# Block attention and two expert layers: four widths for an expert's first products, PSUM tiles cleared in a row and kept for two groups, and twelve transposes at one place

## Chip, cores and metric

The kernel runs on one core of a Trainium2 chip. The metric is the time of one execution on the device, in microseconds (us); the time of a kernel is the median of several executions.

## What is computed

An attention over 4 batches, 8 heads, 576 positions and 64 dimensions (masked, half of the heads local, half strided) gives x with 2304 tokens of 512 dimensions. A first expert layer sends every token to one of 8 experts, which has two matrices, 512 x 1024 and 1024 x 512. A second layer does causal attention once per expert, for 4 experts, and adds up each token's two chosen ones. The change lies in the first expert layer:

```
for s in range(S):
    fresh_e = int(np.argmax(logits[b, s]))
    if s == 0 or local_gate[b, s] < 0.5:
        e = fresh_e
    else:
        e = prev_e if prev_e >= 0 else fresh_e
    prev_e = e
    ...
    h = np.maximum(x[b, s] @ w1[e], 0.0)
    out[b, s] = p[e] * (h @ w2[e])
```

How many tokens an expert gets is known only at run time. On the reference's inputs it is 294, 311, 363, 357, 267, 269, 209 and 234 for experts 0 to 7.

## The kernel before

Every fp32 product is made of three matmuls: both operands are split into a high and a low part (`split`, L118 on ScalarE and L119 on VectorE), and `mm3` (L122 to L124) adds high x high, high x low and low x high in PSUM. The program has three stretches: attention, routing and expert 0 up to about 160 us, the loop over experts 1 to 7 up to about 390 us, and the second layer.

In the loop, one expert `e` (1 to 6) goes through these steps:

- `h_step(e, f)` for f = 0 to 7, one *group* each: 128 of the 1024 inner columns, as the product of `W1` (four tiles of 128 input dimensions) and the expert's transposed tokens `XH[e]`; 4 x 3 = 12 matmuls into a PSUM tile `hp` of 384 columns, one column a token. How many columns are computed is decided on TensorE by a count `CN[e]` that `load_cn` reads: 384, 320 or 256 (`EARLY`). The columns beyond are cleared by `zero` (L849), one bf16 matmul. Then `relu2` (L704 on ScalarE, L705 on VectorE) makes the high and low part of the result from all 384 columns. The tiles `hp` use the PSUM tags s (two buffers), s, xt and lg in turn, so that group f + 4 uses the buffer of group f.
- `split_w2(e, f)` beside it: the high and low part of a 128 x 512 piece of the second matrix.
- `y_step(e, r)` for r = 0, 1, 2, 128 tokens each: 8 x 3 matmuls of 512 columns into `yp`, scaled by ScalarE and scattered to memory by GpSimd. For r = 2 an expert with fewer tokens does a shorter form or clears the tile only.
- Beside `y_step(e, 1)`, `xt_expert(e + 1, [c])` transposes the next expert's gathered tokens, 128 dimensions (c) at a time: three transposes on TensorE into a tile `xp` (L841), and its split into `XH[e + 1]`. `next_w` splits pieces of the next expert's first matrix (`w1h`, `w1l`).

Expert 7 takes another path (`h_late`, `hpl`). TensorE and GpSimd follow the order in which the program is written; ScalarE, VectorE and the DMA queue of SyncE follow an order that a scheduler made from it.

Of the kernel before, what the change touches and what calls it, by code (L numbers as in the profile page):

```python
# [9 lines left out]
FT = mybir.dt.float32  # L10
# [46 lines left out]
def kernel(  # L57
# [19 lines left out]
    DM = H * D  # L77
    NE, _, F = moe_w1.shape
# [3 lines left out]
    CAP = 384  # L82
    RC = CAP // 128
    EARLY = 256
# [8 lines left out]
    def pool(c, name, bufs=1, **kw):  # L93
        return c.enter_context(tc.tile_pool(name=name, bufs=bufs, **kw))
# [56 lines left out]
    def shared(n, shape, dt, name):  # L151
        return sh.tile(shape, dt, name=name, tag=f"sh{n}", bufs=1)
# [568 lines left out]
    for n in range(NU * B):  # L721
# [10 lines left out]
        m = n + 2  # L732
# [13 lines left out]
    for b in range(B):  # L746
        o = 4 * b + 5
        t = (.1, .57, .58, .85, .88, 1.25, 1.58, 1.9, 2.15, 2.5, 2.58) if b < B - 1 else RL
        r = [(logits, (b, (0, 1))), (logits, (b, (2, 3)))]
# [19 lines left out]
    psum = pool(ctx, "psum", space=PSUM)  # L769
# [60 lines left out]
    def xt_expert(e, cs=range(4)):  # L830
        if 0 not in cs:
            pass
        elif e % 2:
            XH[e] = [bp.tile([128, 4, CAP], FR, name=f"xo{n}", tag=f"xo{n}", bufs=1) for n in range(2)]
        else:
            XH[e] = [shared(n, [128, 4, CAP], FR, f"xh{n}") for n in range(2)]
        h, l = XH[e]
        for c in cs:
            p = psum.tile([128, CAP], FT, name="xp", tag="prep", bufs=2)
            for r in range(RC):  # L840
                nc.tensor.transpose(p[:, r * 128:(r + 1) * 128], XG[e, r][:, c * 128:(c + 1) * 128], idf)  # L841
            split(h[:, c], l[:, c], p)

    CN = {}
# [4 lines left out]
    def zero(o):  # L849
        nc.tensor.matmul(o, zb, zb[:, :1].to_broadcast([128, o.shape[1]]), start=True, stop=True)  # L850

    def h_step(e, f):
        nt = EARLY if e == NE - 1 else CAP
        tag = ("s", "s", "xt", "lg")[f % 4]
        p = psum.tile([128, CAP], FT, name="hp", tag=tag, bufs=2 if tag == "s" else 1)[:, :nt]
        xh, xl = XH[e]
        def body(n):
            for c in range(4):
                wh, wl = W1[e, c]
                fs = slice(f * 128, (f + 1) * 128)  # L860
                mm3(p[:, :n], wh[:, fs], wl[:, fs], xh[:, c, :n], xl[:, c, :n], c == 0, c == 3)
            if n < nt:
                zero(p[:, n:])

        if nt > EARLY:
            with tc.If(CN[e] > 320) as q1:
                body(CAP)
            with q1.Else():
                with tc.If(CN[e] > EARLY) as q2:
                    body(320)  # L870
                with q2.Else():
                    body(EARLY)
        else:
            body(nt)
        if f == 0:
            HT[e] = [bp.tile([128, 8, CAP], FR, name=f"h{n}", tag=f"ht{n}", bufs=1) for n in range(2)]
        relu2(HT[e][0][:, f, :nt], HT[e][1][:, f, :nt], p)
# [46 lines left out]
        split(ht[0][:, n * 4:n * 4 + 4], ht[1][:, n * 4:n * 4 + 4], p)  # L924

    def y_step(e, r, beside={}, to=(0, 1)):
        p = psum.tile([128, DM], FT, name="yp", tag=("et", "pv", "lg")[r], bufs=1)
        late = e == 0 and r == 2
        hh, hl = HT["late" if late else e]
        rs = slice(0, 128) if late else slice(r * 128, (r + 1) * 128)  # L930
        def body():
            for f in range(8):
                wh, wl = W2[e, f]
                mm3(p, hh[:, f, rs], hl[:, f, rs], wh, wl, f == 0, f == 7)
                if f in beside:
                    beside[f]()

        def halves():
            for f in range(8):
                for w in range(2):  # L940
                    nc.tensor.matmul(p, HT["hl"][:, f], W2[e, f][w], start=f == w == 0, stop=f == 7 and w == 1)

        half = r == 2 and 0 < e < NE - 1
        if half:
            with tc.If(CN[e] > EARLY + 64) as c:
                body()
            with c.Else():
                with tc.If(CN[e] > EARLY) as c2:
                    halves()
                with c2.Else():  # L950
                    zero(p)
        elif r == 2 and e:
            with tc.If(CN[e] > EARLY) as c:
                body()
            with c.Else():
                zero(p)
        else:
            body()
        if e not in YS:
            YS[e] = shared(4, [128, RC, DM], FT, "y")  # L960
        y = YS[e][:, r]
        nc.scalar.activation(y, p, AF.Copy, scale=pslot[:, r, e:e + 1])  # L962
        if half:
            yb = bp.tile([64, DM], FT, name="yb", tag="hs", bufs=1)
            nc.scalar.activation(yb, p[64:], AF.Copy, scale=both[64:, e:e + 1])
            nc.vector.scalar_tensor_tensor(y[:64], yb, pslot[:64, r, e:e + 1], y[:64], op0=OP.mult, op1=OP.add)
        scatter(y, lambda n: sidx[:, n, r, e:e + 1], to)
# [135 lines left out]
    for e in range(1, NE):  # L1103
        if e + 1 < NE:
            gather(e + 1)
        if e == NE - 1:
            NOV.append(nc.values_load(nov, min_val=0, max_val=(NT - CAP) // 128))
            for f, a, ws in ((h_late, (0, 0), (0, 1, 2)), (h_late, (0,), (3,)), (h_late, (1,), ()),
                             (h_late, (1, 0), (4, 5)), (h_late_t, (0,), ()), (h_late_t, (1,), ()),
                             (h_late_t, (0, 0), ()), (h_late, (0, 1), (6, 7)), (h_late_t, (1, 0), ())):  # L1110
                for w in ws:
                    split_w2(e, w)
                f(e, *a)
            overflow()
            y_step(e, 2)
            y_step(e, 0, to=(0,))
            c_load(0)
            h_late(e, 1, 1)
            scatter(YS[e][:, 0], lambda n: sidx[:, n, 0, e:e + 1], (1,))
            h_late_t(e, 0, 1)  # L1120
            h_late_t(e, 1, 1)
            y_step(e, 1, to=(1,))
            for t in range(5):
                c_t(0, t)
            break
        for f in range(8):
            h_step(e, f)
            split_w2(e, f)
        if e in (1, 3):
            load_cw(e - 1)  # L1130
            load_cw(e)
        HT["hl"] = bp.tile([128, 8, 128], FR, name="h2", tag="hs", bufs=1)
        for x in range(2):
            nc.gpsimd.tensor_copy(HT["hl"][:, :, 64 * x:64 * x + 64], HT[e][x][:, :, EARLY:EARLY + 64])
        load_w2(e + 1)
        for r in range(RC):
            if r == 1:
                load_cn(e + 1)
            y_step(e, r, {2 * c: lambda c=c: xt_expert(e + 1, [c]) for c in range(4)} if r == 1 else {})
            next_w(e + 1, r)  # L1140
        if e + 2 < NE:
            load_w1(e + 2)
# [224 lines left out]
    for b in range(B):  # L1367
        P = TAB[b == B - 1]
        o = 20 * b
        for u in range(10):  # L1370
            pr, i = cunits[10 * b + u][1:]
# [15 lines left out]
    for i in ORD2 or range(len(ev)):  # L1387
        _, f, a = ev[i]
# [31 lines left out]
```

## Time and profile before

| | before |
|---|---|
| median of 3 executions | 600.62 us (600.55 to 603.41) |
| profiled execution | 601.53 us, span of its instructions 599.7 us |
| mean granted TensorE clock | 0.983 |
| TensorE (PE) busy | 566.1 us, 94% |
| VectorE (DVE) busy | 384.8 us, 64% |
| ScalarE (ACT) busy | 349.3 us, 58% |
| GpSimd (POOL) busy | 147.8 us, 25% |

PE stands for TensorE's matmuls, PEld for its weight loads, which lie beside them. Matmuls overlap: a row's second number is the length of an instruction, and what the engine takes per matmul is the distance from one start to the next. In rows of a timeline the columns are start, length, engine, line, operation, the tiles written and read, shapes, and how many instructions are merged in the row.

### The profile page before, as it was taken

The numbers are of one execution on the slowest core, as the hardware profiler recorded it, in microseconds if no ns is written. First come the engines' busy times: TensorE is split into PE (matmuls) and PEld (weight loads), VectorE is DVE, ScalarE is ACT, GpSimd is POOL, SyncE is SP. The second block draws the span as 40 slices with busy tenths as digits, with TensorE's granted clock in tenths as the row PEclk, the third lists the DMA queues.
The fourth block names the chain that finished last, engine by engine and source line by source line (L and its number), as shares of the span: only waits on it lengthen the run. The fifth ranks groups of instructions, "written<-read, shape, count | busy, mean of one in ns | idle before, by whom it ended". The sixth has DMA issues, their size and how long they took to land. (4 is left out here: it accounts for less than half of the span.)

```text
span 599.7 us, 14224 instructions
## 1 busy us (share of the span) xinstructions
PE 566.1 (94%) x5265; PEld 488.3 (81%) x5265; DVE 384.8 (64%) x1135; ACT 349.3 (58%) x868; POOL 147.8 (25%) x229
## 2 busy tenths in 40 slices
PE   7898899879899999999999999998999999999996
PEld 4787787668788898989898987798997997989764
DVE  3456788846474643475555555148897897887891
ACT  2575766641464653455555557335776767767883
POOL 8242223241341423335252534200000000000000
PEclk9699799999999999999999999998999999999999
DMA  9999979440685474584737330331302402302302
GB/s 182 171 242 255 228 184 244 156 147 4 221 283 156 177 236 126 185 263 155 228 131 219 117 144 15 105 108 31 98 18 67 137 19 58 94 37 58 93 18 89
DMA packets 81219, 82.47 MB, mean 138 GB/s; under 512 B 56808, under 2 KB 56808, under 8 KB 80624
## 3 DMA queue, kind: packets, MB, share of 16 engines
q1 hardware_dynamic: 73024, 65.58, 39.8%
q0 software_dynamic: 8112, 15.76, 7.7%
q8 instruction: 55, 0.90, 0.6%
q14 instruction: 28, 0.23, 0.1%
HBM read 62.42 MB, written 21.76 MB: 140 GB/s over the span
## 5 line engine op out<-in xcount | busy, mean ns | idle before, releaser
L196 POOL DMA_INDIRECT yd<-y,sidx x47 | 53.8, 1144 | 82.6 <-ACT y L962 52.3
L119 DVE TENSOR_TENSOR w1l<-w1raw,w1h 128x1024 fp32r<-128x1024 f32 (+1 forms) x44 | 42.3, 986 | 30.5 <-ACT w1h L118 30.5
L1248 ACT ACTIVATE E<-cs,c_mx 128x288 f32<-128x288 f32 (+4 forms) x96 | 45.7, 481 | 17.1 <-DVE c_mx L1246 14.6
L122 PE MATMUL yp<-w2h,h 128*128 128x512 f32 x128 | 52.8, 412 | 0.4 <-ACTq L972 0.4
L1278 POOL MEMSET E<- 128x128 f32 x40 | 8.3, 209 | 180.0 <-PE cet L1297 84.9
L118 ACT ACTIVATE w1h<-w1raw 128x1024 fp32r<-128x1024 f32 (+1 forms) x44 | 34.3, 828 | 28.6 <-PE hp L124 18.5
L124 PE MATMUL yp<-w2h,h 128*128 128x512 f32 x128 | 50.3, 393 | 0.0
L123 PE MATMUL yp<-w2l,h 128*128 128x512 f32 x128 | 50.0, 390 | 0.0
L119 DVE TENSOR_TENSOR w2l<-w2raw,w2h 128x512 fp32r<-128x512 f32 x56 | 35.7, 685 | 12.0 <-ACT w2h L118 5.8
L122 PE MATMUL qkp<-y,cw 128*128 128x288 f32 x128 | 39.1, 306 | 0.5 <-DVE y L119 0.5
L1241 PE MATMUL cs<-qkt 128*128 128x288 f32 (+4 forms) x192 | 38.5, 319 | 1.1 <-ACT E L1248 0.9
L1246 DVE TENSOR_REDUCE c_mx<-cs 128x1 f32<-128x288 f32 (+4 forms) x80 | 37.7, 484 | 1.2 <-PE cs L1241 0.7
L118 ACT ACTIVATE w2h<-w2raw 128x512 fp32r<-128x512 f32 x56 | 32.4, 631 | 9.4 <-PE yp L124 4.5
L124 PE MATMUL qkp<-y,cw 128*128 128x288 f32 x128 | 37.8, 295 | 0.0
L123 PE MATMUL qkp<-y,cw 128*128 128x288 f32 x128 | 37.7, 294 | 0.0
L705 DVE SCALAR_TENSOR_TENSOR h<-hp,h 128x384 fp32r<-128x384 f32 x48 | 25.0, 552 | 14.5 <-ACT h L704 14.5
L962 ACT ACTIVATE y<-yp,pslot 128x512 f32<-128x512 f32 x22 | 14.9, 682 | 31.5 <-PE yp L124 22.9
L1292 PE MATMUL cet<-idf,E 128*128 128x128 f32 x160 | 28.3, 279 | 5.0 <-ACT et L115 2.1
L122 PE MATMUL hp<-xo,w1h 128*128 128x320 f32 (+1 forms) x96 | 31.7, 331 | 0.0
L1241 PEld LDWEIGHTS cs<-qkt 128*128 128x128 f32 x192 | 28.7, 193 | 3.2 <-ACT E L1248 2.5
L190 POOL DMA_INDIRECT xg<-xd,gidx x24 | 24.4, 1017 | 26.1 <-DVE gidx L648 19.1
L122 PE MATMUL hp<-xh,w1h 128*128 128x384 f32 (+2 forms) x96 | 30.8, 321 | 0.0
(364 smaller groups left out, 1722.7 us busy)
## 6 DMA issues: line engine op xcount, KB each, us to landing
w1raw<-in_moe_w_dram SPq DMA_DIRECT2D x32, 512.0 KB
w2raw<-in_moe_w_dram SPq DMA_DIRECT2D x56, 256.0 KB
yr<-yd SPq DMA_DIRECT2D x20, 256.0 KB
qkt<-qkt SPq DMA_DIRECT2D x8, 576.0 KB
out_dram<-co SPq DMA_DIRECT2D x16, 256.0 KB
raw<-in_q_dram SPq DMA_DIRECT2D x16, 144.0 KB
raw<-in_k_dram SPq DMA_DIRECT2D x16, 144.0 KB
raw<-in_q_dram SPq DMA_DIRECT2D x8, 288.0 KB
```

The costliest lines, as they stand in the source:

```text
L118: nc.scalar.activation(hi, src, AF.Copy)
L119: (eng or nc.vector).tensor_tensor(lo, src, hi.bitcast(FT), op=OP.subtract)
L122: nc.tensor.matmul(o, ah, bh, start=start, stop=False, **kw)
L123: nc.tensor.matmul(o, ah, bl, start=False, stop=False, **kw)
L124: nc.tensor.matmul(o, al, bh, start=False, stop=stop, **kw)
L190: nc.gpsimd.indirect_dma_start(out=t, out_offset=None, in_=xd[:rows], in_offset=bass.IndirectOffsetOnAxis(ap=gidx[:, r, e:e + 1], axis=0))
L196: nc.gpsimd.indirect_dma_start(out=yds[n], out_offset=bass.IndirectOffsetOnAxis(ap=ix(n), axis=0), in_=y, in_offset=None, bounds_check=yds ...
L705: nc.vector.scalar_tensor_tensor(lo, p, 0.0, hi.bitcast(FT), op0=OP.max, op1=OP.subtract)
L1241: nc.tensor.matmul(o[:, h - h0], T[:, h, q0:q0 + 128], T[:, 2 + 2 * x + h, k0:k1], start=x == 0, stop=x == 1, skip_group_check=True)
L1246: nc.vector.tensor_reduce(mx[:, n, h0:h0 + G], o, axis=AX.X, op=OP.max, negate=True)
L1248: nc.scalar.activation(E[:, h, k0:k1], o[:, h - h0], AF.Exp, bias=mx[:, n, h:h + 1], accum_out=sm[:, n, h:h + 1])
L1292: nc.tensor.transpose(p[:, kt * 128:kt * 128 + 128], E[:, kt * 128:kt * 128 + 128], idf)
```

## The change

- The widths are 256, 288, 320 and 384, chosen by two comparisons in every case (before, the 384-wide arm was chosen after one).
- An expert's four tiles `hp` are allocated once, at f = 0. If the width is below 384, four zeros in a row clear the columns beyond it in all four tiles, ahead of the first group's products; group f + 4 writes to the same tile again, and its cleared columns stay as they are.
- All twelve transposes of the next expert stand after f = 3 of `y_step(e, 1)`, instead of three each after f = 0, 2, 4 and 6; from expert 2 on their tiles use the tags prep and s in turn (two buffers each) instead of prep alone.
- `y_step(e, 2)` uses the PSUM tag et (pv for expert 7) instead of lg.

```
-            p = psum.tile([128, CAP], FT, name="xp", tag="prep", bufs=2)
+            p = psum.tile([128, CAP], FT, name="xp", tag=("prep", "s")[c % 2 if e > 1 else 0], bufs=2)
...
+    HP = {}
+
     def h_step(e, f):
         nt = EARLY if e == NE - 1 else CAP
-        tag = ("s", "s", "xt", "lg")[f % 4]
-        p = psum.tile([128, CAP], FT, name="hp", tag=tag, bufs=2 if tag == "s" else 1)[:, :nt]
+        if f == 0:
+            for i, tag in enumerate(("s", "s", "xt", "lg")):
+                HP[i] = psum.tile([128, CAP], FT, name="hp", tag=tag, bufs=2 if tag == "s" else 1)
+        p = HP[f % 4][:, :nt]
         xh, xl = XH[e]
         def body(n):
+            if n < nt and f == 0:
+                for i in range(4):
+                    zero(HP[i][:, n:])
             for c in range(4):
                 wh, wl = W1[e, c]
                 fs = slice(f * 128, (f + 1) * 128)
                 mm3(p[:, :n], wh[:, fs], wl[:, fs], xh[:, c, :n], xl[:, c, :n], c == 0, c == 3)
-            if n < nt:
-                zero(p[:, n:])
+
+        def pick(ws):
+            if len(ws) == 1:
+                body(ws[0])
+                return
+            m = len(ws) // 2
+            with tc.If(CN[e] > ws[m - 1]) as q:
+                pick(ws[m:])
+            with q.Else():
+                pick(ws[:m])
 
         if nt > EARLY:
-            with tc.If(CN[e] > 320) as q1:
-                body(CAP)
-            with q1.Else():
-                with tc.If(CN[e] > EARLY) as q2:
-                    body(320)
-                with q2.Else():
-                    body(EARLY)
+            pick((EARLY, 288, 320, CAP))
...
-        p = psum.tile([128, DM], FT, name="yp", tag=("et", "pv", "lg")[r], bufs=1)
+        p = psum.tile([128, DM], FT, name="yp", tag=("et", "pv", "pv" if e == NE - 1 else "et")[r], bufs=1)
...
-            y_step(e, r, {2 * c: lambda c=c: xt_expert(e + 1, [c]) for c in range(4)} if r == 1 else {})
+            y_step(e, r, {3: lambda: xt_expert(e + 1)} if r == 1 else {})
```

How the change moves instructions, at three places. In an expert's first group, here one of an even expert's (xh_ are its tokens, w1h and w1l the weights), TensorE before, from the head of the group:

```order
L866 COMPARE_AND_BRANCH
L122 MATMUL hp<-xh_5981,w1h 128x384
...
L866 UNCONDITIONAL_BRANCH
L869 COMPARE_AND_BRANCH
L122 MATMUL hp<-xh_5981,w1h 128x320
...
L124 MATMUL hp<-xh_5981,w1l 128x320
L850 LDWEIGHTS zb
L850 MATMUL hp<-zb 128x64
L869 UNCONDITIONAL_BRANCH
```

and with the change, from the head of the group and then from the arm of 288 on:

```order
L875 COMPARE_AND_BRANCH x2
L122 MATMUL hp<-xh_6470,w1h 128x384
...
L875 UNCONDITIONAL_BRANCH
L875 COMPARE_AND_BRANCH
L850 LDWEIGHTS zb
L850 MATMUL hp<-zb 128x96
...
L122 MATMUL hp<-xh_6470,w1h 128x288
L123 MATMUL hp<-xh_6471,w1h 128x288
L124 MATMUL hp<-xh_6470,w1l 128x288
...
L875 UNCONDITIONAL_BRANCH
```

The zero has moved from behind the group's products to a row of four (two of its eight rows are shown) ahead of the first group's; the groups after the first have none.

TensorE in `y_step(5, 1)`, before:

```order
L122 MATMUL yp<-w2h,h_5576 128x512
L123 MATMUL yp<-w2l,h_5576 128x512
L124 MATMUL yp<-w2h,h_5577 128x512
L841 MATMUL xp<-idf,xg 128x128 x3
L122 MATMUL yp<-w2h,h_5576 128x512
...
```

and with the change:

```order
L122 MATMUL yp<-w2h,h_5986 128x512
L123 MATMUL yp<-w2l,h_5986 128x512
L124 MATMUL yp<-w2h,h_5987 128x512
L841 MATMUL xp<-idf,xg 128x128 x12
L122 MATMUL yp<-w2h,h_5986 128x512
...
```

Before, a piece of three comes after the first, third, fifth and seventh three products; with the change all twelve come after the fourth.

ScalarE in expert 5's eight groups (w2h is a split of its second matrix, w1h one of the next expert's first, h the relu of a group), before:

```order
L704 ACTIVATE h_5576<-hp 128x384 x3
L118 ACTIVATE w2h<-w2raw_5345 128x512
L704 ACTIVATE h_5576<-hp 128x384
...
L118 ACTIVATE w1h<-w1raw 128x1024
L704 ACTIVATE h_5576<-hp 128x384
L118 ACTIVATE w1h<-w1raw 128x1024
L704 ACTIVATE h_5576<-hp 128x384 x3
L118 ACTIVATE w1h<-w1raw 128x1024 x2
```

and with the change:

```order
L704 ACTIVATE h_5986<-hp 128x384 x4
L118 ACTIVATE w2h<-w2raw_5724 128x512
...
L118 ACTIVATE w2h<-w2raw_5729 128x512
L118 ACTIVATE w1h<-w1raw 128x1024
L704 ACTIVATE h_5986<-hp 128x384 x4
L118 ACTIVATE w1h<-w1raw 128x1024 x3
```

The relu of group 4 stood between two splits of w1; now groups 4 to 7 follow one another, behind five splits of w2 and one of w1.

## Rows read from the trace of the kernel before

**Rows 1.** Busy time by engine, the stretch 160 to 390 us (length, busy us, instructions, PEclk, DMA, GB/s).

```profile
160.00:390.00 230.00, 227.33 (x1263) 198.38 (x1261) 123.37 (x183) 123.13 (x211) 84.30 (x79) 1.00 0.53 172
```

**Rows 2.** TensorE's waits, 160 to 390 us, the longest (in total, times, longest).

```profile
PE hpt L915 <- ACT hs L905: 1.4, 2, 1.2
```

**Rows 3.** TensorE's instructions grouped by line and shape (count | busy us, mean ns).

```profile
L122 PE MATMUL hp<-xo,w1h 128*128 128x320 f32 x64 | 21.0, 328 | 0.0
...
L122 PE MATMUL hp<-xh,w1h 128*128 128x320 f32 x32 | 10.5, 328 | 0.0
...
L850 PE MATMUL hp<-zb 128*128 128x64 bf16 x24 | 4.9, 203 | 0.0
...
L850 PE MATMUL hp<-zb 128*128 128x128 bf16 x8 | 1.8, 229 | 0.0
```

**Rows 4.** Timeline of TensorE, a group of 320 columns in expert 1.

```profile
174.86 0.40 PE L122 MATMUL hp<-xo,w1h 128*128 128x320 f32 x1
175.09 0.31 PE L123 MATMUL hp<-xo,w1h 128*128 128x320 f32 x1
...
176.56 0.31 PE L124 MATMUL hp<-xo,w1l 128*128 128x320 f32 x1
176.71 0.20 PE L850 MATMUL hp<-zb 128*128 128x64 bf16 x1
176.75 0.40 PE L122 MATMUL hp<-xo,w1h 128*128 128x320 f32 x1
```

**Rows 5.** Timeline of TensorE, 288-wide products of the second layer.

```profile
390.90 0.29 PE L123 MATMUL qkp<-y,cw 128*128 128x288 f32 x1
...
392.22 0.29 PE L124 MATMUL qkp<-y,cw 128*128 128x288 f32 x1
```

**Rows 6.** Timeline of TensorE, one zero of 512 columns and two in a row.

```profile
359.90 0.39 PE L850 MATMUL yp<-zb 128*128 128x512 bf16 x1
...
360.37 0.40 PE L123 MATMUL hpl<-w1l,xo 128*128 128x512 f32 x1
...
362.93 0.61 PE L850 MATMUL hpl<-zb 128*128 128x512 bf16 x2
...
363.60 0.40 PE L123 MATMUL hpl<-w1l,xo 128*128 128x512 f32 x1
```

**Rows 7.** Timeline of TensorE, fifteen bf16 matmuls of 48 columns, before the loop.

```profile
146.74 0.55 PE L636 MATMUL slot<-r_vo,r_rm 128*128 128x48 bf16 x15
147.13 0.36 PE L122 MATMUL hpe<-xh,w1h 128*128 128x256 f32 x1
```

**Rows 8.** Timeline of VectorE, the last split of expert 2's transposed tokens.

```profile
200.53 0.56 DVE L119 TENSOR_TENSOR xh<-xp,xh 128x384 fp32r<-128x384 f32 x1 [0.80 <-ACT xh L118]
```

**Rows 9.** Timeline of TensorE, first products of two groups in a row, expert 2.

```profile
204.16 0.34 PE L122 MATMUL hp<-xh,w1h 128*128 128x384 f32 x1
...
206.24 0.34 PE L122 MATMUL hp<-xh,w1h 128*128 128x384 f32 x1
```

**Rows 10.** TensorE's transposes: timeline in expert 1, sixteen in a row, and grouped.

```profile
194.32 0.49 PE L841 MATMUL xp<-idf,xg 128*128 128x128 f32 x3
...
194.88 0.39 PE L123 MATMUL yp<-w2l,h 128*128 128x512 f32 x1
...
387.32 1.91 PE L1047 MATMUL yt<-idf,yr 128*128 128x128 f32 x16
...
L841 PE MATMUL xp<-idf,xg 128*128 128x128 f32 x84 | 13.7, 272 | 0.0
```

**Rows 11.** Timeline of TensorE, a group of 256 columns in expert 6.

```profile
339.73 0.23 PE L850 MATMUL hp<-zb 128*128 128x128 bf16 x1
...
341.27 0.23 PE L850 MATMUL hp<-zb 128*128 128x128 bf16 x1
341.31 0.36 PE L122 MATMUL hp<-xh,w1h 128*128 128x256 f32 x1
```

**Rows 12.** DMA queues, 160 to 390 us: the queue of instructions (packets, MB, share).

```profile
q8 instruction: 23, 0.38, 0.7%
```

## The prediction

> **What bounds the kernel now.** I read the windows first: from 160 to 390 us, the stretch of the expert loop that the change touches, TensorE is busy for 227.33 of 230 us at a granted clock of 1.00 [rows 1]. The reader should see two things there. ScalarE and VectorE are busy for about 123 us each and the DMA engines for about half, so nothing else is near a bound on average, and a microsecond of TensorE work taken out of this stretch is a microsecond of the kernel unless another engine then comes late. The list of TensorE's waits says how little slack there is to win otherwise: its longest entry in the stretch is 1.4 us in all [rows 2]. So the sum is about TensorE's start-to-start times, not about the durations that the profile prints: a 320-wide matmul has a duration of 0.31 us but the next one starts 0.147 us later, since the matmuls overlap. All prices below are such distances.
>
> **Who executes what.** The trace shows which arm each expert took. There are 96 320-wide matmuls on each of the three product lines, 64 reading the odd experts' tokens and 32 the even ones' [rows 3], at 4 per group: 24 groups, three experts. These are experts 1, 5 (odd) and 4 (even); experts 2 and 3 run 384 wide and expert 6 runs 256 wide. The 24 clearing matmuls of 64 columns and the 8 of 128 agree [rows 3]. The trace alone can't say which of the three would fit 288. The reference on its inputs can: its routing gives 311 tokens to expert 1, 267 to expert 4 and 269 to expert 5 (363, 357 and 209 for 2, 3 and 6). So 4 and 5 go to the new 288 arm and the others keep theirs.
>
> **Part 1, the width.** A 320-wide group: ten distances take 1.47 us, from 175.09 to 176.56, 0.147 us each [rows 4]. A 288-wide product exists already in the second layer's projections, with the same operand types: ten distances from 390.90 to 392.22, 0.132 us each [rows 5]. The change makes 16 groups of 12 matmuls narrower: 192 x 0.0145 to 0.015 = 2.8 us. All of it is TensorE time with nothing beside it to hide it. Readers of the results (ScalarE's and VectorE's relu and split) still work on 384 columns, so their work is what it was.
>
> **Part 2, the zeros.** A 320-wide group takes 1.89 us from its first matmul at 174.86 to the next group's first at 176.75; twelve matmuls of 0.147 explain 1.76, so one zero costs 0.126 us, though its columns alone are few [rows 4]. The rows show where it goes: the zero starts 0.15 after the last matmul, the next matmul 0.04 after the zero, but the one after that 0.23 later instead of 0.147. Before, 32 such zeros run: 4.0 us. After, 16 run, four in a row at an expert's start, in experts 1, 4, 5 and 6. What the second to fourth in a row cost, the trace shows only for other shapes, and I bound it. Above: the full 0.126 each. Below: what the columns take. Two 512-wide zeros in a row move the second following matmul from 0.47 us after the first zero (359.90 to 360.37) to 0.67 (362.93 to 363.60) [rows 6], so the second cost 0.20, its 512 columns and no more. Fifteen bf16 matmuls of 48 columns took 0.39 us, 0.026 each [rows 7]. I take the low end, because both rows are bf16 matmuls following one another and the extra in [rows 4] comes after the zero, at the return to the fp32 products, which happens once per row of zeros. Scaled from 0.20 per 512 columns and not below 0.026: 0.027, 0.040 and 0.053 us for 64, 96 and 128 columns. A row of four then costs 0.126 + 3 x that: 0.21 in expert 1, 0.25 in 4 and 5, 0.28 in 6, 0.99 in all. Saved: 4.0 - 1.0 = 3.0 us (2.0 with the high end).
>
> The zeros now stand at the head of the first group, before any product, and one of them writes the tiles of groups 1, 2 and 3, so a late reader of any of the four tiles would hold up the start. These readers are the relu and split of groups 4 to 7 of the expert before, which lie ahead of its three y steps, and, new, the splits of two transposed tiles, which now use the same PSUM buffers. In the kernel before, the last such split ended at 201.09 [rows 8], 3.1 us before the next expert's first product at 204.16 [rows 9], and in the change the last transposes stand nine products of y step 1 earlier, some 2 us. I cost this wait at nothing.
>
> **Part 3, the comparisons.** An expert of 384 columns now passes two comparisons per group instead of one. With one comparison and a jump between groups, the 384-wide groups show no gap: one group takes 2.08 us, from 204.16 to the next one's first product at 206.24, which is 0.173 per matmul with the boundary in it [rows 9], and 320 wide at 0.147 scales to 0.176. With two comparisons and a jump, in the 320-wide groups, the matmul comes 0.04 after the zero [rows 4]. TensorE's queue covers them, so I cost the 16 additional ones at nothing. The Trainium skill, Advanced Engine Details and Errata, section Control Flow Timing, puts a compare-and-branch at about 108 ns; if these stood on the path, 16 of them would be an estimated 1.7 us, and the sum -4.2 instead of -5.9 us. The trace does not bear that out.
>
> **Part 4, the transposes.** Three transposes between products cost 0.33 us: from their start at 194.32 to the second product behind them at 194.88 are 0.56 us, where two products alone would have been 0.23 apart [rows 10]. That is 0.11 each. Sixteen in a row took 1.91 us, of which 0.27 is the length of the last [rows 10], so fifteen distances of 0.109. Twelve at one place instead of four times three: six experts x 12 x 0 to 0.003 = 0 to 0.2 us; I take 0.1. With four buffers instead of two the twelve do not wait for a split; the gathered tokens are needed later than before, not earlier.
>
> **Part 5, the order on ScalarE and VectorE.** The relu of group 4 no longer stands between two weight splits, and experts 3 to 6 do four relus in a row. I cost this at nothing, and the cover is this: the expert of 256 columns already runs groups 1.54 us apart (its zeros at 339.73 and 341.27) [rows 11] with the same relu and split work per group, and the longest entry of TensorE's waits in the whole loop is one for another tile [rows 2]. The new 288-wide groups come every 12 x 0.132 = 1.59 us, which is slower than that. y step 2 now takes the buffer of y step 0, which ScalarE reads while y step 1 runs, 24 products of 0.23 us.
>
> **Sum.** 2.8 + 3.0 + 0.1 = 5.9 us off TensorE. What follows the loop waits for the last expert's products, so I let it move up as a whole. Against the profiled execution of 601.53 us (span 599.7) that is 595.6; this execution lies 0.9 above the median of the runs, 600.62, and against that median it is **594.7 us**. A measurement of this kernel can tell about 0.5%, 3.0 us, from no change.
>
> **Rivals.**
> *Zeros at full price.* If each of the four zeros costs 0.126, the saving is 4.9: 595.7 us. For it: the trace has no row of two narrow zeros. Against: [rows 6, 7].
> *Saving handed back.* The narrower experts bring ScalarE's and VectorE's splits of the weights nearer to their use, and the new order puts up to five weight splits before the relu of group 4. If TensorE waited for about half of what was taken out, 597.6 us. Against: expert 6's pace [rows 11].
> *It doesn't do what it says.* If experts 4 and 5 took the 320 arm after all (their counts on the chip over 288), only zeros and transposes remain, 3.0 + 0.1, and the time is 597.5 us. The counts speak against it.
> *Slower: TensorE's instructions come late.* A group now holds four arms of 24 matmul and weight-load instructions, where it held three, and is over sooner, so jumps reach further and instructions are consumed faster per microsecond. Their fetches show in the queue of the kind "instruction": 23 packets in the stretch, 0.7% of sixteen engines' 230 us, which is 1.1 us each [rows 12]. If a third of the 48 groups had to wait for one, that is 16 x 1.1 = 18 us: 600.6 - 5.9 + 18 = 613 us; from six waits on the change loses. It decides as soon as a jump lands on instructions not yet fetched. Against: the 256-wide groups jump past two arms, about 50 instructions, and the matmul behind them starts 0.04 after the zero, without a gap [rows 11], and the fetches of now, about one in 10 us, cost TensorE no wait near that size [rows 2]. The Trainium skill, Runtime: NRT & Kernel Launch, section Instruction fetch mechanics, states this mechanism: a taken branch to a target outside what is fetched has to wait for a DMA. No row here shows such a wait.
>
> **How the numbers follow.** Forecast 0.62 (its own range 594 to 595.5); full-price zeros 0.13; saving handed back 0.11; 288 not taken 0.04; slower by fetches or by a wait that I overlooked 0.07; the rest, 0.03, no effect for another reason. The first two lie below 597.6, the bound of 0.5%, and so does about a third of the third: faster 0.79. The third's rest, the fourth and the last make 0.14 for no change, and 0.07 is left for slower. The range reaches from 593.3 (a run-to-run shift and the ends of the width price) to 598.4, which takes in all but the cases at or above no change.
>
> **What would show it.** In the profile after: 64 matmuls of hp 288 wide on each of the three product lines, and 32 of 320; 16 zeros of hp in four rows of four; the 288-wide groups 1.59 us apart, the 320-wide ones 1.76 instead of 1.89 and the 256-wide ones 1.42 instead of 1.54; expert 2's and 3's groups still 2.08; TensorE's waits in the loop no longer than 3 us. A group of 288 at 1.7 or more, gaps without a releaser at group boundaries, or a wait of the row of zeros for VectorE would prove the respective step wrong.

## The result, and the profile after

The changed kernel took 593.92 us, the median of 4 executions (592.26 to 601.71), beside 601.17 us of 4 of the kernel before. The ratio is 0.9863, 95% interval 0.9815 to 0.9911; it leaves out the execution of 601.71 us, which was in the chip's slower state. A second series (6 executions beside 29) gave 0.9884, interval 0.9838 to 0.993. The 594.7 us of the prediction are a ratio of 0.990, inside both intervals but at the cautious end of the first: the change gave more than the sum said. On the prediction's base of 600.62 us the first ratio is 592.4 us, below its range of 593.3 to 598.4, and the second is 593.7. The executions of one kernel lie several us apart, so what each part gave can't be read from times. It can be read from the traces, because the loop repeats to 0.02 us in two traces of the changed kernel.

First the windows of the kernel before, cut at the first product of expert 0's last y step and at the first projection of the second layer (length, busy us of PE, PEld, DVE, ACT and POOL, PEclk, DMA share, GB/s):

```profile
0.00:166.33 166.33, 145.95 (x2585) 118.88 (x2586) 103.39 (x348) 89.02 (x207) 57.19 (x114) 0.95 0.73 184
166.33:390.67 224.34, 222.28 (x1236) 194.16 (x1234) 120.15 (x180) 119.10 (x205) 82.93 (x79) 1.00 0.52 170
390.67:599.70 209.03, 197.87 (x1448) 175.29 (x1448) 161.22 (x609) 141.16 (x457) 7.69 (x37) 0.99 0.24 66
```

and of the changed kernel, cut at the same instructions:

```profile
0.00:165.76 165.76, 145.65 (x2585) 118.17 (x2586) 103.16 (x348) 89.12 (x207) 57.25 (x114) 0.97 0.72 184
165.76:383.39 217.63, 215.13 (x1216) 190.90 (x1218) 119.28 (x180) 117.61 (x205) 79.37 (x79) 1.00 0.55 175
383.39:591.50 208.11, 196.54 (x1448) 173.74 (x1448) 160.88 (x609) 141.13 (x457) 7.69 (x37) 1.00 0.24 66
```

The span fell by 8.2 us (599.7 to 591.5). The loop, the middle row, gave 6.71 of them, at a granted clock of 1.00 in both. The other 1.5 lie in stretches whose instructions the change leaves as they were: 0.57 ahead of the loop, 0.92 behind it, both with a higher granted clock in the second trace.

What the loop is made of now. The products' groups by line and shape, and the zeros (count | busy us, mean ns), answer to [rows 3]:

```profile
L122 PE MATMUL hp<-xo,w1h 128*128 128x320 f32 x32 | 10.0, 311 | 0.0
...
L122 PE MATMUL hp<-xo,w1h 128*128 128x288 f32 x32 | 9.6, 299 | 0.0
L122 PE MATMUL hp<-xh,w1h 128*128 128x288 f32 x32 | 9.5, 298 | 0.0
...
L850 PE MATMUL hp<-zb 128*128 128x96 bf16 x8 | 0.7, 208 | 0.0
L850 PE MATMUL hp<-zb 128*128 128x128 bf16 x4 | 0.4, 222 | 0.0
L850 PE MATMUL hp<-zb 128*128 128x64 bf16 x4 | 0.3, 196 | 0.0
```

So one expert of 320 is left, an odd and an even one run 288 wide, and 16 zeros are left of 32, as forecast. TensorE's timeline at the start of expert 4 and at one of its later groups (start, length, instruction), which answers to [rows 4, 5]:

```profile
271.34 0.35 PE L850 MATMUL hp<-zb 128*128 128x96 bf16 x4
271.51 0.38 PE L122 MATMUL hp<-xh,w1h 128*128 128x288 f32 x1
271.73 0.29 PE L123 MATMUL hp<-xh,w1h 128*128 128x288 f32 x1
...
273.19 0.30 PE L122 MATMUL hp<-xh,w1h 128*128 128x288 f32 x1
...
274.79 0.30 PE L122 MATMUL hp<-xh,w1h 128*128 128x288 f32 x1
```

The row of four zeros costs 0.26 us (271.34 to the second product at 271.73 is 0.39, less one distance of 0.13), where four single ones cost 0.5. A group takes 1.60 us, 0.133 per product with the comparison and the jump in it; no gap stands at its head.

Cut by steps at the first instruction of each, the loop of the kernel before, of the change (both traces of it) and of the three single parts below (us; h: an expert's eight groups, y: the three y steps behind them with the transposes):

| step | before | change | change again | 288 alone | zeros alone | transposes alone |
|---|---|---|---|---|---|---|
| h 1 | 15.04 | 14.29 | 14.29 | 15.05 | 14.30 | 15.04 |
| y 1 | 16.06 | 15.87 | 15.87 | 16.05 | 15.98 | 15.94 |
| h 2 | 16.64 | 16.64 | 16.64 | 16.64 | 16.64 | 16.64 |
| y 2 | 17.82 | 17.71 | 17.71 | 17.83 | 17.83 | 17.71 |
| h 3 | 16.65 | 16.65 | 16.65 | 16.64 | 16.64 | 16.65 |
| y 3 | 17.81 | 17.69 | 17.69 | 17.82 | 17.81 | 17.70 |
| h 4 | 15.01 | 13.05 | 13.05 | 13.67 | 14.29 | 15.01 |
| y 4 | 16.08 | 15.87 | 15.87 | 16.08 | 16.00 | 15.96 |
| h 5 | 15.05 | 13.05 | 13.06 | 13.67 | 14.29 | 15.05 |
| y 5 | 16.05 | 15.87 | 15.86 | 16.09 | 15.99 | 15.94 |
| h 6 | 12.20 | 11.20 | 11.20 | 12.20 | 11.20 | 12.20 |
| y 6 | 12.47 | 12.28 | 12.28 | 12.47 | 12.37 | 12.37 |
| whole loop | 224.34 | 217.63 | 217.65 | 221.77 | 220.75 | 223.67 |

The rest of the loop is expert 0's last y step ahead of these and expert 7 behind them. Expert 7 gives and takes up to 0.8 us between neighbouring steps; the whole rest is the same in all six to about 0.1.

### The profile page after: what moved, and what is told of

It reads as the page before. It is cut to its first block, busy times and chain, and to the rows that moved or that the text cites. A ratio compares the mean times of both kernels' runs of the same rounds, so it can differ in the third digit from the quotient of the medians.

```text
span 591.5 us, 14206 instructions
## 1 busy us (share of the span) xinstructions
PE 557.3 (94%) x5246; PEld 482.8 (82%) x5249; DVE 383.3 (65%) x1135; ACT 347.9 (59%) x868; POOL 144.3 (24%) x229
## 5 line engine op out<-in xcount | busy, mean ns | idle before, releaser
L196 POOL DMA_INDIRECT yd<-y,sidx x47 | 50.8, 1082 | 91.7 <-ACT y L971 53.3
L122 PE MATMUL yp<-w2h,h 128*128 128x512 f32 x128 | 50.7, 396 | 1.3 <-ACTq L981 1.3
L124 PE MATMUL yp<-w2h,h 128*128 128x512 f32 x128 | 50.0, 391 | 0.0
L704 ACT ACTIVATE h<-hp 128x384 fp32r<-128x384 f32 x48 | 21.3, 490 | 21.1 <-PE hp L124 14.1
L122 PE MATMUL hp<-xo,w1h 128*128 128x320 f32 (+2 forms) x96 | 30.3, 315 | 0.0
```

The costliest lines, as they stand in the source:

```text
L122: nc.tensor.matmul(o, ah, bh, start=start, stop=False, **kw)
L124: nc.tensor.matmul(o, al, bh, start=False, stop=stop, **kw)
L196: nc.gpsimd.indirect_dma_start(out=yds[n], out_offset=bass.IndirectOffsetOnAxis(ap=ix(n), axis=0), in_=y, in_offset=None, bounds_check=yds ...
```

## The experiments

### The parts, one at a time

The kernel before with the fourth width alone:

```
-            with tc.If(CN[e] > 320) as q1:
...
+            pick((EARLY, 288, 320, CAP))
```

> The kernel before with the 288-wide arm alone; the zeros stay behind every group, the transposes where they were. Measured in the trace from the first product of expert 0's last y step to the first projection of the second layer (224.34 us before, 217.63 with the whole change, -6.71). My sum says -2.8 us there, all of it in experts 4 and 5 (a 288-wide group with its zero 1.72 us), with every other expert's groups as before. Rival, that the additional arm and comparisons cost something: less than -2.4, and groups of experts 2 and 3 over 2.08 us.

The loop took 221.77 us, 2.57 less. Experts 4 and 5 gave 1.34 and 1.38, and nothing else moved by more than 0.04 in any h or y step. 2.72 us is the part's worth; the comparisons and the longer jumps cost experts 2 and 3 nothing (16.64). Ratio 0.9963 (0.9928 to 0.9998).

The changed kernel without its two other parts: the zeros in a row and kept (with y step 2 on the tag et, as in the change), three widths, and the transposes where they were:

```
-            p = psum.tile([128, CAP], FT, name="xp", tag=("prep", "s")[c % 2 if e > 1 else 0], bufs=2)
+            p = psum.tile([128, CAP], FT, name="xp", tag="prep", bufs=2)
...
-            pick((EARLY, 288, 320, CAP))
+            pick((EARLY, 320, CAP))
...
-            y_step(e, r, {3: lambda: xt_expert(e + 1)} if r == 1 else {})
+            y_step(e, r, {2 * c: lambda c=c: xt_expert(e + 1, [c]) for c in range(4)} if r == 1 else {})
```

> The change without the 288-wide arm and with the transposes where they were: tiles cleared in a row and kept, y step 2 on the other buffer. My sum: -3.1 us in that stretch, expert 6 giving 0.7. The trace after showed expert 6 giving 1.0, its 256-wide matmuls 0.113 us apart instead of 0.118. Theory A: a zero in each group keeps the products behind it slower, so without zeros 0.113 again and -3.4 in all. Theory B: 0.113 belongs to something else of the change; then 0.118 and -3.1.

3.59 us less, so theory A: expert 6 gives 1.00 here too, 1, 4 and 5 give 0.74, 0.72 and 0.76, 3.22 in all. Another 0.32 comes from the y steps of these four experts (0.06 to 0.10 each, none in 2 and 3), 3.54 for the part: the zero behind the eighth group also delayed the first products of the y step. From the first of them to the second is 0.32 us in the kernel before and 0.23 here, in expert 1:

```profile
188.10 0.48 PE L122 MATMUL yp<-w2h,h 128*128 128x512 f32 x1
188.42 0.39 PE L123 MATMUL yp<-w2l,h 128*128 128x512 f32 x1
```

```profile
188.01 0.40 PE L122 MATMUL yp<-w2h,h 128*128 128x512 f32 x1
188.24 0.39 PE L123 MATMUL yp<-w2l,h 128*128 128x512 f32 x1
```

Ratio 0.996 (0.9928 to 0.9992).

The transposes at one place, and nothing else of the change:

```
-            p = psum.tile([128, CAP], FT, name="xp", tag="prep", bufs=2)
+            p = psum.tile([128, CAP], FT, name="xp", tag=("prep", "s")[c % 2 if e > 1 else 0], bufs=2)
...
+            y_step(e, r, {3: lambda: xt_expert(e + 1)} if r == 1 else {})
```

> The kernel before with the twelve transposes at one place and their tiles on two tags, nothing else. My prediction took 0.1 us for this part; the trace after shows the y steps 0.11 to 0.2 us shorter per expert, 1.0 us in all. Theory A: the products behind each group of transposes are slower (0.231 to 0.233 us apart instead of 0.227), so one place instead of four gives -1.0 us by itself. Theory B: the shorter y steps come from the rest of the change; then -0.1 to -0.2.

0.67 us less, 0.10 to 0.12 in each of the six y steps: between the two theories, and by itself 0.57 more than I had taken. The trace of the kernel before shows what I had cut off too early, here between two places of three transposes in y step 1 of expert 5:

```profile
325.43 0.49 PE L841 MATMUL xp<-idf,xg 128*128 128x128 f32 x3
325.68 0.48 PE L122 MATMUL yp<-w2h,h 128*128 128x512 f32 x1
325.99 0.39 PE L123 MATMUL yp<-w2l,h 128*128 128x512 f32 x1
...
326.92 0.40 PE L124 MATMUL yp<-w2h,h 128*128 128x512 f32 x1
327.15 0.49 PE L841 MATMUL xp<-idf,xg 128*128 128x128 f32 x3
```

and of the change, in expert 3, from the twelve transposes to the sixteenth product behind them:

```profile
261.85 1.47 PE L841 MATMUL xp<-idf,xg 128*128 128x128 f32 x12
263.08 0.48 PE L122 MATMUL yp<-w2h,h 128*128 128x512 f32 x1
263.40 0.39 PE L123 MATMUL yp<-w2l,h 128*128 128x512 f32 x1
...
266.58 0.39 PE L122 MATMUL yp<-w2h,h 128*128 128x512 f32 x1
```

Before, three transposes and six products take 1.72 us (325.43 to 327.15); six products undisturbed are 1.36 (0.227 each), so the transposes cost 0.36, not the 0.33 that [rows 10] give up to the second product: the five distances behind that one are 0.232 instead of 0.227 (325.99 to 327.15). Four times 0.36 is 1.44. Twelve and fifteen products take 4.73 us now, less 3.40 is 1.33. That is the 0.11. Ratio 0.9969 (0.9941 to 0.9997).

The whole change once more:

> The change once more, to see what of the -8.2 us of its profile belongs to it. Theory A: the loop gives -6.7 in every profile, and the remaining 1.5 us come from where the granted clock happens to fall (second layer: 0.94 before and 1.00 after in its first 30 us, 0.86 us of the difference) and from the attention stretch; then the ratio over five rounds lies at 0.988 to 0.990. Theory B: the whole 8.2 us belong to the change; ratio 0.986 and again a clock of 1.00 behind the loop.

The loop took 217.65, to 0.02 us what it took the first time. The rest did not repeat: 166.7 us ahead of it, 208.4 behind it. In the first 30 us of the second layer the granted clock was 0.94 in the trace of before and 1.00 in that of the change:

```profile
390.00:420.00 30.00, 27.32 (x203) 26.76 (x202) 19.33 (x67) 13.75 (x43) 0.74 (x4) 0.94 0.27 74
```

```profile
382.70:412.70 30.00, 27.27 (x213) 26.55 (x212) 20.23 (x72) 14.60 (x46) 0.77 (x4) 1.00 0.30 85
```

In both, TensorE stands idle for 2.1 us there, for the softmax of the first block; in the first trace the products behind that idle time run at the lower of the clock's two levels, 1.2 GHz, for 3.4 us (415.03 to 418.44), in the second they stay at 2.4 GHz. In the traces of the kernel before, the change and the three single parts, the part behind the loop took 207.7 to 209.0 us and the part ahead of it 165.65 to 168.93, with a clock of 0.92 to 0.99 ahead of it, in kernels whose instructions are the same in both parts. Over all fourteen traces of this document these 30 us have a clock of 0.94 in seven, where the part behind the loop took 209.0 to 209.5 us, and of 1.00 in the other seven, the change's two among them, where it took 207.7 to 208.4. The kernel with the zeros alone is among the first, those with 288 or the transposes alone among the second. So theory A for the 1.5 us: they are not the change's. Why the clock falls behind that idle time in some executions and not in others is open. The ratio of this series can't decide it, since 0.986 lies in its interval too.

### Two supports taken away

Transposes at one place, but their tiles on prep alone (this kernel and the next ran once, so the loop of the trace is compared; its granted clock was 1.00 in both):

```
-            p = psum.tile([128, CAP], FT, name="xp", tag=("prep", "s")[c % 2 if e > 1 else 0], bufs=2)
+            p = psum.tile([128, CAP], FT, name="xp", tag="prep", bufs=2)
```

> The change with the twelve transposes on the tag prep alone, two buffers. The third piece of three then waits for the split of the first (ScalarE 0.49 and VectorE 0.56 us), the fourth for the second's: theory +0.7 to 1.0 us in the y step of each of six experts, the loop 222 to 224 us. Rival: the splits follow the transposes closely enough; +0.2 or less in each.

227.71 us: five of the six y steps take 1.20 to 1.23 us more, expert 1's 2.83 more, 8.9 in all, and expert 1's groups 1.22 (below). TensorE's waits name it (in total, times, longest):

```profile
PE xp L841 <- DVE xh L119: 4.1, 4, 1.5
PE xp L841 <- DVE xo L119: 1.7, 2, 0.8
```

The third piece of three waits for the first one's split, as expected, and the price was above the range. With the wait in expert 6, which the profile lists without a releaser (0.8), these are 6.6 us of idle time; the other 2.2 of the 8.9 are not shown as waits. Without the second tag the move of the transposes would have turned the whole change into a loss (217.65 + 8.9 = 226.6 against 224.34).

y step 2 back on lg:

```
-        p = psum.tile([128, DM], FT, name="yp", tag=("et", "pv", "pv" if e == NE - 1 else "et")[r], bufs=1)
+        p = psum.tile([128, DM], FT, name="yp", tag=("et", "pv", "pv" if e == NE - 1 else "lg")[r], bufs=1)
```

> The change with y step 2 back on the PSUM tag lg (experts 1 to 6). The row of zeros at the next expert's start then also writes the tile that ScalarE still reads for y step 2 (two reads of 0.69 us behind the last product). Theory: about 1.3 us of waiting at the start of experts 4, 5 and 6 and 0.7 of expert 1, none for 2 and 3, whose groups without zeros reach that tile later: the loop 217.65 + 4.6 = 222 us, half of what the whole change gains. Rival: expert 1 none at all if its predecessor's y step stands elsewhere; then +3.9.

223.16 us, 5.5 more; 0.83 in expert 1, 1.51, 1.49 and 1.68 in 4, 5 and 6, nothing in 2 and 3: the pattern that was expected, 0.9 us dearer. The row of zeros stands and waits for ScalarE's reads:

```profile
PE hp L850 <- ACT yb L974: 4.0, 3, 1.3
PE hp L850 <- ACT y L971: 0.7, 1, 0.7
```

So a line of the diff that looks like bookkeeping carries 5.5 of 6.7 us. In the prediction I costed the row of zeros' waits at nothing, which held, since the change had moved this reader out of the way.

### More widths, and the rival that waits behind them

Five widths:

```
-            pick((EARLY, 288, 320, CAP))
+            pick((EARLY, 272, 320, 368, CAP))
```

> The change with five widths, 256, 272, 320, 368 and 384, instead of four; the counts put experts 4 and 5 (267, 269 tokens) at 272 and experts 2 and 3 (363, 357) at 368. From the distances measured (288: 0.1335, 320: 0.1465, 384: 0.173 us, that is 0.0133 more for each 32 columns) 272 would be 0.127 and 368 0.167 us: experts 4 and 5 each 12.4 us instead of 13.05, experts 2 and 3 each 16.2 instead of 16.64 with their row of zeros; the loop 217.65 - 2.1 = 215.5 us. Rival (instructions come late behind longer jumps over five arms): gaps without a releaser at the heads of groups, some 1 us each, and a loop above 217.65.

The loop 216.19 us. Experts 4 and 5 took 12.12 and 12.31, 2 and 3 16.41 and 16.42 (0.23 less each instead of 0.44, as a product of 368 came every 0.169 us instead of 0.167), but expert 1 took 14.86 instead of 14.29, with the first gap without a releaser at a group's head, 0.29 us, and expert 6 took 11.31 instead of 11.20. Ratio 0.9857 (0.9823 to 0.989), which can't be told from the change's.

Nine widths:

```
-            pick((EARLY, 288, 320, CAP))
+            pick(tuple(range(EARLY, CAP + 1, 16)))
```

> The same with nine widths, 256 to 384 in steps of 16: the same widths are taken as with five, but a group holds nine arms of 24 instructions and its jumps pass up to eight of them, and three or four comparisons stand ahead of a group. My theory: the loop as with five widths, to 0.2 us. Rival: if TensorE's instructions come late, waits in most of the 48 groups, from 1 us each; with a block of instructions per 16 KB packet used up in about one group instead of two and a half, the loop 10 to 50 us longer.

Seven widths:

```
-            pick((EARLY, 288, 320, CAP))
+            pick((216, EARLY, 272, 312, 360, 368, CAP))
```

> Seven widths, 216, 256, 272, 312, 360, 368 and 384: expert 1 (311 tokens) takes 312, expert 2 368, expert 3 360, experts 4 and 5 272, expert 6 (209) 216. Against five widths: expert 1 96 x 0.0033 = -0.3 us, expert 3 -0.3 us. Expert 6: if a 256-wide matmul's 0.113 us still go by its columns, 216 gives 0.097 and -1.6 us; if they are the weight load's (the transposes, 128 columns, are 0.109 apart), 0 to -0.4 us. The loop 215.5 - 0.6 - 0.4 = 214.5 us by the second, 213.3 by the first.

The rival, clearly: 280.74 us with nine and 248.77 with seven, ratios 1.0886 (1.0807 to 1.0964) and 1.048 (1.0441 to 1.0518). Nine widths are 64 us above five, more than the rival's 10 to 50. Expert 6's question was answered beside it: where no gap stands, its 216-wide products come 0.112 us apart (357.21 to 359.00, 16 distances), so below 256 columns hardly anything is saved. The loop's granted clock fell to 0.95 and 0.98, as TensorE stands idle in it again and again. With nine widths the groups of every expert took 23.5 to 25.7 us, whatever they compute, experts 3 and 4 at a clock of 1.00. TensorE's waits in the loop, with nine:

```profile
PE hp L122 <- issue: 36.3, 25, 3.8
PE hp L122 <- DVE w2l L119: 9.5, 5, 2.1
```

and the timeline at one group's head in expert 3:

```profile
279.37 0.33 PE L124 MATMUL hp<-xo,w1l 128*128 128x368 f32 x1
281.49 0.44 PE L122 MATMUL hp<-xo,w1h 128*128 128x368 f32 x1 [1.79 <-issue]
```

"issue" is idle time in which the engine waited for nothing that the profile shows. (The waits laid to VectorE's w2l stand at the same kind of place, where no product of the group reads w2l, which belongs to the y step.) Whether it was the odd widths or the arms that are only passed, the next run tells. The change with three widths more that no expert takes:

```
-            pick((EARLY, 288, 320, CAP))
+            pick((EARLY, 288, 304, 320, 336, 352, CAP))
```

> The change with three more widths that no expert takes (304, 336 and 352 beside 256, 288, 320 and 384): every matmul that runs is the change's own, and only the unused arms and one more comparison are new. With five, seven and nine widths the loop took 216.2, 248.8 and 280.7 us, and with nine every expert's eight groups took 23.5 to 25.7 us whatever their width, 1780 instructions each, which is seven packets of 16 KB at 256 instructions and 3.5 us a packet. Theory: it is the arms that are passed, not the widths: 1390 instructions in an expert's groups, 5.4 packets, 17 to 21 us for experts 1, 4, 5 and 6 and 16.7 to 18.6 for 2 and 3, the loop 240 to 250 us, and some 10 packets of instructions more over the whole run than with four widths and 6 matmuls' worth of nothing else. Rival: the odd widths (216, 312, 360, 272) were slow; then the loop stays at 217.7.

251.71 us in the one trace, 34 more, though the matmuls that run are the change's:

```profile
165.03:416.74 251.71, 225.56 (x1220) 195.40 (x1218) 119.81 (x180) 117.96 (x205) 78.87 (x79) 0.98 0.47 153
```

The groups took 20.27, 21.29 and 21.00 us in experts 1, 4 and 5, 17.96 and 17.88 in 2 and 3, 14.05 in 6 (whose y steps then took 5.3 us more). So it isn't the odd widths; the arms that are passed cost it. Two other causes can be held against the traces. The clock was at its lower level for 10.2 us of this loop, which is at most 5 of the 34 us, and experts 1, 3 and 6 took 6.0, 1.2 and 2.9 us longer at a clock of 1.00. The one comparison more does not explain it either: expert 6 passes two, as in the change, and with five widths experts 2 and 3 passed three without a gap.

The packets of the queue of instructions come with the arms, here of the change and of this kernel (whole run: packets, MB, share):

```profile
q8 instruction: 59, 0.97, 0.7%
```

```profile
q8 instruction: 74, 1.21, 0.8%
```

Over the whole run they count 54 with three widths, 59 with four (the change), 64 with five, 74 with seven in either kernel, 85 with nine: some 5.2 for every arm. The expectation had said 10 more for three arms, it is 15. An arm has 48 x 24 = 1152 instructions, so a packet of 16 KB brings about 220 of them, with the jumps not counted. And they come slowly. Expert 3's groups in the kernel with nine widths, 23.54 us, in the list of queues (packets, MB, share of 16 engines):

```profile
q1 hardware_dynamic: 432, 0.79, 10.1%
q8 instruction: 7, 0.11, 2.0%
```

Seven packets in 23.54 us are 3.4 us from one to the next, though each is under way for only 1.1 us (2.0% of 16 x 23.54, by 7) and the DMA engines are nearly free. In none of the fourteen traces do two of these packets start less than 2.9 us apart; why they come no faster is open. That the gaps are waits for them shows in their times: in the loop with nine widths 31 products at a group's head follow idle time of more than 0.25 us, and every one of them starts 1.4 to 2.6 us behind the landing of such a packet, none sooner. So with many arms TensorE goes at the pace of its instructions, one packet in some 3.4 us. The four arms of the change are 8 x 4 x 24 = 768 instructions in an expert's eight groups, at 220 a packet 3.5 packets, an estimated 12 us, and the groups take 11.2 to 16.6. That is on the edge. It works, I think, because the y steps behind are long and have few instructions (one to three packets each in the traces); no run here tests that. The Trainium skill, Runtime: NRT & Kernel Launch, section Instruction fetch mechanics, says that instructions come in blocks of 16 KiB, 256 each, and that a taken branch to a target outside the blocks at hand has to wait for a fetch. The traces agree with the block's size within some 15% and with a wait behind a branch. The same section of the Trainium skill calls the crossing of a block mostly hidden; in the traces it is hidden with 1.6 us of work for about 100 instructions, as in the change, and it isn't with 1.4 to 2.0 us for about 220, as with nine widths.

### Versions near the edge

```
-            pick((EARLY, 288, 320, CAP))
+            pick((EARLY, 272, 320, CAP))
```

> Four widths again, 256, 272, 320 and 384: experts 4 and 5 at 272, all else as in the change. From the run with five widths a 272-wide matmul comes every 0.123 us: experts 4 and 5 take 12.1 us each instead of 13.05, the loop 217.65 - 1.9 = 215.8 us, a little below five widths (216.19), with no gap at a group's head, since a group passes as many instructions as in the change but is 7% shorter: 2.5 groups of 1.48 us a packet, 3.7 us, still above 3.5. If the packets already decide there, up to 1 us of gaps in experts 4 and 5. Ratio to the kernel before 0.983 to 0.987.

217.41 us. Expert 4 gave what was expected, 12.12, expert 5 12.31. But expert 1, in which nothing had been changed, took 15.72 instead of 14.29, 1.2 us of it in one gap:

```profile
PE hp L122 <- issue: 1.2, 1, 1.2
```

The kernel with one tag, also of four widths, shows such a gap of 0.94 us in expert 1; the two traces of the change and that with lg do not. Both gaps, and that of five widths, end 1.9 us behind the landing of a packet of instructions. So with four arms expert 1 sometimes waits for a packet. Ratio 0.9892 (0.9856 to 0.9928).

Three widths, none of which is 256:

```
-            pick((EARLY, 288, 320, CAP))
+            pick((272, 320, CAP))
```

> The change with three widths, 272, 320 and 384, so that a group passes 72 instructions where the change passes 96. Experts 4, 5 and 6 at 272: 12.1 us each (13.05, 13.05 and 11.20 in the change), the rest as in the change, so the loop 217.65 - 0.9 - 0.9 + 0.9 = 216.7 us. If the packets of instructions cause the gap of 1.2 us in expert 1 that the run with 272 as one of four widths showed (and the 0.2 us in its expert 5), no gap at any group's head here, expert 1 at 14.3 and expert 5 at 12.1 us, and some 5 packets fewer than the change's 59. If that gap has another cause (a late weight, the run's own chance), it can come back: expert 1 above 15 us.

216.91 us, and no gap in the loop's groups: expert 1 14.29, experts 4, 5 and 6 12.13, 12.31 and 12.12, and 54 packets. The 0.2 us of expert 5 came again, so they have nothing to do with packets: its 272-wide products are 0.125 us apart, expert 4's 0.123; why is open. Ratio 0.9868 (0.9822 to 0.9915), median 594.6 of 6. No version of these four (change, five widths, 272, three) can be told from another by its time. By the trace three widths are worth 0.7 us more than the change's four, with the distance to the edge besides.

## What the prediction had right, and the terms that it sized too small

The mechanism held and the sum was too small: 6.7 us left the loop, where the sum said 5.9. The step that failed is the price of what stands between the products, in two terms. Part 2 put the zeros at 3.0 us, and they gave 3.54 alone; part 4 put the transposes at 0.1, and they gave 0.67 alone. The range had no room for that: its faster end, 593.3, allowed for a run-to-run shift and the width alone. Term by term:

- **The bound** was right: the loop is TensorE's distances, and 6.7 us taken out of it came out of the span. The forecast was 5.9.
- **Part 1, the width**: 2.8 forecast, 2.72 alone. A product of 288 in the loop is 0.133 us, as in the second layer.
- **Part 2, the zeros**: 3.0 forecast, 3.54 alone. The price of a row of four was right (0.21 us in expert 1, 0.26 in 4, 0.30 in 6, forecast 0.21, 0.25 and 0.28), and with it the choice of the low end; the rival of full price falls. What was too small is the price of the single zeros. The step "one zero costs 0.126 us" left out two things: the products of the y step behind the eighth zero (0.32 in all), and, in the 256-wide expert, products that are 0.005 us further apart as long as a zero stands in each group (1.00 instead of 0.71).
- **Part 3, the comparisons**: nothing, as forecast: experts 2 and 3 took 16.64 us with one comparison per group and with two. The 108 ns that the Trainium skill gives for one (Advanced Engine Details and Errata, section Control Flow Timing) are not on the path here.
- **Part 4, the transposes**: 0.1 forecast, 0.67 alone. The step "0.56 us, where two products alone would have been 0.23 apart" ended at the second product; the five distances behind it are longer too.
- **Part 5, ScalarE and VectorE**: no wait came in the groups or y steps of experts 1 to 6. The longest of TensorE's waits in the loop is one of 1.3 us, in expert 7.
- **The sum**: the parts alone add up to 6.93, and to 6.71 together, since a zero costs less behind 288-wide groups: 0.62 between the kernel with 288 alone and the change in each of experts 4 and 5, instead of 0.74.
- **The rest of the first profile's 8.2 us**, 1.5, was no part of the sum and is not the change's; it goes with where the granted clock fell in one trace and not in the other.
- **The slower rival** had the right mechanism and the wrong terms. I priced a wait at 1.1 us, the length of a packet, but they come 3.4 us apart and waits are up to 4 us; and I let it decide by the reach of a single jump, where it is instructions per microsecond. What I held against it, 50 instructions jumped without a gap, says nothing about a mean rate. The kernel stands close to it: in two other kernels with four arms expert 1 waited once, five arms cost it 0.6 us there, and seven cost the loop 31 to 34 us.

## What to carry to other kernels

An If per group costs nothing on TensorE until the arms that are passed, taken or not, use up instructions faster than they are fetched, here 16 KB in some 3.4 us; then further arms cost more than the widths gave here (16 us each from five to nine), so count instructions per microsecond over all arms before adding one. A small matmul of another kind between products costs more than the gap that it makes: measure up to where the old distance is back, or compare a whole stage with and without it. When tiles are cleared ahead of time, look for who still reads them at that point: here one change of a PSUM tag decided 5.5 of 6.7 us.

## What the runs showed of the hardware that was not expected

The rate of instructions above: a packet of 16 KB in some 3.4 us, and never two within 2.9. And a distance that depends on what came before: 256-wide products come 0.118 us apart in the kernel before (ten distances),

```profile
339.97 0.28 PE L123 MATMUL hp<-xh,w1h 128*128 128x256 f32 x1
...
341.15 0.28 PE L124 MATMUL hp<-xh,w1l 128*128 128x256 f32 x1
```

and 0.113 in the change, without a zero in the groups (twelve distances):

```profile
330.52 0.28 PE L122 MATMUL hp<-xh,w1h 128*128 128x256 f32 x1
...
331.88 0.28 PE L122 MATMUL hp<-xh,w1h 128*128 128x256 f32 x1
```

The kernel with the zeros alone has it too (11.20 us for expert 6) and those with 288 or the transposes alone don't (12.20), so it is the zeros that bring it about. Products of 320 columns show no such difference, 0.147 us with and without. Why 256 does is open.
